# Sharing a score block between the two heads of a pair, split by early and late keys, in a fused linear-attention and MLP kernel

## Chip, cores and metric

The kernel runs on one core of a Trainium2 chip. The metric is device time in microseconds (us). All times quoted are medians of runs in the undisturbed ("fast") state; one run of the kernel before (240.27 us, in the round with the copies on ACT) was slow and is left out of the ratios. The engines are called PE (matrix engine), PEld (its weight loads), DVE (vector engine), ACT (scalar engine), POOL (GpSimd) and SP (which issues transfers).

## The reference

Two stages run one after the other. The first is causal linear attention with a decay per head. The second is a two-layer MLP without biases.

```
# q, k, v: (4, 8, 768, 64)   batch, heads, tokens, width;   lam: one decay per head
# blocks of 64 tokens; rel = i - j
Dmask = where(rel >= 0, lam ** rel, 0)
out   = ((q @ k.T) * Dmask) @ v  +  (q * lam**(pos+1)) @ state     # inside the block + state
state = lam**64 * state + (k * lam**(63-pos)).T @ v
x = attention output as (3072, 512)
h = x @ w_in                                   # 512 -> 2048
g = where(h >= 1, h, where(h <= -1, 0, (h + 1)**2 / 4))
y = g @ w_out                                  # 2048 -> 512
```

## The kernel before

The kernel works in chunks of 128 tokens: 24 chunks, six per batch element. Decay is folded into q and k by tables of `lam**pos` and `lam**-pos` ("casts", mostly on POOL), so that the mask inside a chunk is a plain causal 0/1 mask. Heads are handled in four pairs, since two heads of width 64 fill 128 rows.

For each chunk, PE transposes q and k. DVE copies the transposed k into `kbd`, one 128x128 weight per head, whose other head's rows are zero. PE makes a score block per head (`ps`, two groups of four because only one PSUM bank is free). DVE masks each group (`sc`). PE multiplies with v (`vi`, one weight per head, the other head's columns zero) and adds the state term, all into `po`.

```
def cast_v(c):                               # ACT: v to bf16, straight into the weight layout
    nc.scalar.copy(out=v_out(vi[c % NV]), in_=qkv_ld[c, 2]...)

def f_kb(c, hi):                             # DVE, two per chunk
    nc.vector.tensor_copy(kbd[c % NKB][HD[hi], :, hi, :], ptt[c][HD[hi], 1])

def f_s(c, g):                               # PE, g = 0, 1: 4 matmuls of 128 columns
    pst[c, g] = pp_s.tile([128, 4, 128], F32, ...)           # one buffer
    for j in range(2):
        for hi in range(2):
            nc.tensor.matmul(pst[c, g][:, 2*j+hi, :], lhsT=kbd[c % NKB][:, 2*g+j, hi, :],
                             rhs=qT[c][:, 2*g+j, :], start=True, stop=True)

def f_m(c, g):                               # DVE, mask: 128x512
    nc.vector.tensor_tensor(sc_sb[c][:, 4*g:4*g+4, :], pst[c, g], _bc(causal, 1, 4), op=AX.mult)

def f_o(c):                                  # PE: state term, then two heads, per pair
    for hp in range(HP):
        if cb > 0: nc.tensor.matmul(po[:, hp], lhsT=ubd[...][:, hp, :], rhs=qT[c][:, hp, :], ...)
        for hi in range(2):
            nc.tensor.matmul(po[:, hp], lhsT=vi[c % NV][:, hp, hi]..., rhs=sc_sb[c][:, 2*hp+hi, :], ...)
```

The MLP runs beside this: first layer `ph` on PE, `r` on ACT, three DVE operations `t`, `w`, `gT` on 128x1024, second layer `py` on PE, `osb` on ACT.

Every operation is registered with an engine and a cost in nanoseconds. When the program is built, a list scheduler simulates the engines with these costs and emits each engine's instructions in the simulated order. At run time each engine takes its instructions in that order.

```
add(("kb", c, hi), "DVE", 365, lambda: f_kb(c, hi), needs...)
add(("s", c, h), "PE", mm(*[128] * 4), lambda: f_s(c, h), needs...)     # mm(n) = n / 2.4 + 3 ns
add(("m", c, h), "DVE", 690, lambda: f_m(c, h), needs...)
...                                          # cut: the other operations, loads, weights
run_plan({"PE": 7000, "ACT": 6500, ...})     # simulate, then emit in the simulated order
```

## Time and profile before

| | before |
|---|---|
| median of 3 runs | 238.5 us (238.32 to 239.11) |
| span of the profiled run | 234.8 us |
| PE / DVE / ACT / POOL busy | 213.8 / 160.3 / 123.4 / 59.4 us |

First the page's busy line, and the line of shares, by engine, of the chain that ended last:

```profile
PE 213.8 (91%) x1876; PEld 137.1 (58%) x1904; DVE 160.3 (68%) x274; ACT 123.4 (53%) x216; POOL 59.4 (25%) x64
...
PE 75%; DVE 16%; ACT 3%; DMA 2%; issue 2%; SPq 0%; ACTq 0%
```

The table of windows splits this by time. Each row gives the stretch, its length, and then the busy time (with instruction counts) of PE, PEld, DVE, ACT and POOL, the granted PE clock, the DMA share and the GB/s:

```profile
22.00:30.00 8.00, 6.83 (x59) 4.26 (x58) 3.24 (x6) 4.41 (x9) 0.00 (x0) 1.00 1.10 198
...
46.00:70.00 24.00, 23.84 (x298) 18.61 (x299) 16.56 (x27) 13.00 (x24) 9.98 (x10) 1.00 0.94 199
70.00:94.00 24.00, 22.57 (x329) 19.45 (x331) 23.35 (x43) 16.59 (x32) 14.76 (x13) 1.00 1.06 216
94.00:134.00 40.00, 39.27 (x425) 27.94 (x431) 30.70 (x53) 23.74 (x42) 10.75 (x10) 1.00 0.81 182
134.00:190.00 56.00, 55.58 (x401) 31.47 (x408) 39.80 (x72) 31.06 (x53) 6.13 (x6) 1.00 0.09 34
```

Window length less PE's busy time is PE's idle time: 1.4 us from 70 to 94 us, 0.7 us from 94 to 134 us and 0.4 us from 134 to 190 us. In the first of these DVE is full too (23.35 of 24 us).

The list of waits on PE names engine, waiting group, releaser, total us, times and longest:

```profile
PE ps L252 <- DVE qT L236: 2.5, 3, 1.7
...
PE ps L252 <- DVE sc L258: 0.8, 3, 0.3
```

The second score group of a chunk needs the PSUM bank that the first mask empties, so it waits for DVE. Here that wait is 0.8 us in the whole run.

Last, two kinds of group lines, with count, total busy and mean ns. The first is the mask; the other two are single `t` operations, the first with a cast on POOL beside it, the second with none:

```profile
L258 DVE TENSOR_TENSOR sc<-ps,causal 128x512 bf16<-128x512 f32 x48 | 33.0, 687 | 19.0 <-PE ps L252 18.8
...
L311 DVE TENSOR_SCALAR t_464<-r 128x1024 bf16<-128x1024 bf16 x1 | 1.7, 1661 | 0.0
...
L311 DVE TENSOR_SCALAR t_486<-r 128x1024 bf16<-128x1024 bf16 x1 | 0.4, 420 | 0.0
```

The same operation takes 420 ns or up to 1661 ns. All that take over 450 ns overlap a cast on POOL.

### The profile page before, as it was taken

Reading aid. Unit: us, or ns where it says so; the run is one execution under the profiler, and the core shown is the slowest. Engines: PE = TensorE matmul, PEld = TensorE weight load, DVE = VectorE, ACT = ScalarE, POOL = GpSimd, SP = SyncE. Lnnn points to the kernel's source line nnn. Section 1 sums busy time; section 2 is a strip of 40 time slices with the busy share of each in tenths; the row PEclk is TensorE's granted clock in tenths of the full one; section 3 lists DMA queues with packets and bytes.
Section 4 is the critical chain, followed back from the end, with each engine's and each line's share of the span. In section 5 each row is a group of like instructions: output and inputs, shape, how many; then the busy total and the mean of one; then the engine's idle time right before and its main releaser. Section 6 shows DMA issues by size and latency. Waiting matters only on the chain.

```text
span 234.8 us, 4665 instructions
## 1 busy us (share of the span) xinstructions
PE 213.8 (91%) x1876; PEld 137.1 (58%) x1904; DVE 160.3 (68%) x274; ACT 123.4 (53%) x216; POOL 59.4 (25%) x64
## 2 busy tenths in 40 slices
PE   0487997999997999999999999999999999999993
PEld 0476633575896997777765455555555454444441
DVE  7587399957499999885776876876766835545300
ACT  3456566243577766666566366566455354544110
POOL 6562071061366548303303403302000000000000
PEclk9999999999999999999999999999999999999999
DMA  6999969986999999899993011011011011110212
GB/s 139 220 212 200 192 112 185 196 162 186 247 201 218 227 221 206 191 243 228 230 255 81 19 45 37 12 45 47 0 45 47 0 45 47 45 43 2 92 51 83
DMA packets 82725, 29.67 MB, mean 126 GB/s; under 512 B 75536, under 2 KB 79632, under 8 KB 82704
## 3 DMA queue, kind: packets, MB, share of 16 engines
q1 hardware_dynamic: 78336, 25.17, 48.2%
q0 software_dynamic: 4224, 4.19, 11.1%
q8 instruction: 15, 0.25, 0.4%
q14 instruction: 6, 0.05, 0.1%
q10 hardware_dynamic: 144, 0.00, 0.0%
HBM read 27.27 MB, written 6.29 MB: 143 GB/s over the span
## 4 chain that ended last, share of the span: by engine, by line
PE 75%; DVE 16%; ACT 3%; DMA 2%; issue 2%; SPq 0%; ACTq 0%
PE py L323 33%; PE ph L295 26%; PE ps L252 5%; DVE gT L315 4%; PE pt L229 4%; PE po L268 4%; DMA x2f<-in_v_dram 2%; DVE sc L258 2%; PE pu L242 2%; PE po L265 2%; ACT r L303 1%; DVE kbd_121 L232 1%; PE ph L288 1%; DVE kbd_120 L232 1%; DVE qT L236 1%
## 5 line engine op out<-in xcount | busy, mean ns | idle before, releaser
L303 ACT ACTIVATE r<-ph,one 128x512 bf16<-128x512 f32 x94 | 64.1, 687 | 57.6 <-PE ph L295 40.9
L295 PE MATMUL ph<-xT,w_in_sb 128*128 128x128 bf16 (+1 forms) x744 | 93.1, 269 | 1.0 <-ACT r L303 0.4
L323 PE MATMUL py<-w_out_sb,gT 128*128 128x512 bf16 x364 | 91.5, 379 | 0.9
L295 PEld LDWEIGHTS <-w_in_sb 128*128 128x128 bf16 x752 | 53.0, 98 | 28.0 <-issue 1.4
L323 PEld LDWEIGHTS <-gT 128*128 128x128 bf16 x384 | 35.4, 98 | 33.3 <-DVE gT L315 0.2
L219 POOL TENSOR_TENSOR ks<-x1f,tab_k 128x512 bf16<-128x512 f32 x21 | 24.0, 1141 | 93.0 <-DMA x1f<-in_k_dram 38.9
L258 DVE TENSOR_TENSOR sc<-ps,causal 128x512 bf16<-128x512 f32 x48 | 33.0, 687 | 19.0 <-PE ps L252 18.8
L219 POOL TENSOR_TENSOR qs<-x0f,tab_q 128x512 bf16<-128x512 f32 x23 | 25.8, 1123 | 7.0 <-DMA x0f<-in_q_dram 6.9
L328 ACT COPY osb<-py 128x512 f32<-128x512 f32 x24 | 14.1, 586 | 20.6 <-PE py L323 20.0
L275 ACT CAST xT<-po 128x512 bf16<-128x512 f32 x24 | 14.0, 585 | 11.9 <-PE po L268 11.8
L242 PEld LDWEIGHTS <-ks 128*128 128x128 bf16 x80 | 6.2, 105 | 9.7 <-DVE ks L219 7.1
L229 PE MATMUL pt<-ident,ks 128*128 128x128 bf16 x96 | 10.1, 232 | 0.1
L229 PE MATMUL pt<-ident,qs 128*128 128x128 bf16 x96 | 10.0, 231 | 0.0
L229 PEld LDWEIGHTS <-ks 128*128 128x128 bf16 x96 | 7.7, 106 | 3.3 <-issue 0.3
L252 PE MATMUL ps<-qT,kbd_121 128*128 128x128 bf16 x64 | 6.8, 229 | 3.0 <-DVE qT L236 1.7
L242 PE MATMUL pu<-vi_126,ks 128*128 128x128 bf16 x24 | 2.5, 232 | 7.7 <-ACT vi_126 L223 7.7
L236 DVE COPY qT<-pt 128x512 bf16<-128x512 bf16 x20 | 8.5, 425 | 0.3
L252 PEld LDWEIGHTS <-kbd_121 128*128 128x128 bf16 x64 | 4.9, 102 | 5.8 <-DVE kbd_121 L232 2.6
L252 PE MATMUL ps<-qT,kbd_120 128*128 128x128 bf16 x64 | 6.8, 229 | 1.4 <-ACT qT L236 1.1
L232 DVE COPY kbd_120<-pt 64x512 bf16<-64x512 bf16 x16 | 6.7, 418 | 1.7 <-PE pt L229 0.9
L252 PE MATMUL ps<-qT,kbd_122 128*128 128x128 bf16 x64 | 6.5, 225 | 1.3 <-DVE qT L236 0.8
L252 PEld LDWEIGHTS <-kbd_120 128*128 128x128 bf16 x64 | 4.8, 102 | 3.8 <-DVE kbd_120 L232 1.8
(207 smaller groups left out, 246.4 us busy)
## 6 DMA issues: line engine op xcount, KB each, us to landing
x1f<-in_k_dram SPq DMA_DIRECT2D x24, 256.0 KB, 4.6
x0f<-in_q_dram SPq DMA_DIRECT2D x24, 256.0 KB, 4.8
x2f<-in_v_dram SPq DMA_DIRECT2D x24, 256.0 KB, 4.7
out_dram<-osb SPq DMA_DIRECT2D x24, 256.0 KB, 2.0
w_in_sb<-in_moe_w_in_dram POOLq DMA_DIRECT2D x4, 512.0 KB, 8.3
w_out_sb<-in_moe_w_out_dram POOLq DMA_DIRECT2D x4, 512.0 KB, 8.3
lam_b<-in_lam_dram ACTq DMA_DIRECT2D x1, 4.0 KB, 3.3
```

The source lines that it names most:

```text
L219: eng.tensor_tensor(t, qkv_ld[c, x], _bc(tab[:, c % NCB, :], 2, D), op=AX.mult)
L229: nc.tensor.transpose(out=ptt[c][:, i, hp, :], in_=pair(x[c], hp), identity=ident)
L232: nc.vector.tensor_copy(kbd[c % NKB][HD[hi], :, hi, :], ptt[c][HD[hi], 1])
L236: (nc.scalar.copy if e == "ACT" else nc.vector.tensor_copy)(qT[c], ptt[c][:, 0])
L242: nc.tensor.matmul(pu[0][:, hp, :], lhsT=pair(ks[c], hp), rhs=v_pair(vi[c % NV], hp), start=(c % NCB == 0 and hp == 0), stop=True, skip_gr ...
L252: nc.tensor.matmul(pst[c, g][:, 2 * j + hi, :], lhsT=kbd[c % NKB][:, 2 * g + j, hi, :], rhs=qT[c][:, 2 * g + j, :], start=True, stop=True)
L258: nc.vector.tensor_tensor(sc_sb[c][:, 4 * g:4 * g + 4, :], pst[c, g], _bc(causal, 1, 4), op=AX.mult)
L275: nc.scalar.copy(out=xT[sx][:, :, off:off + C], in_=pot[c])
L295: nc.tensor.matmul(ph[:, j * m:(j + 1) * m], lhsT=w_in_sb[:, ko, (ni + j) * 128:(ni + j + 1) * 128], rhs=xT[s][:, ko, part * m:(part + 1) ...
L303: nc.scalar.activation(out=r_t[grp][:, i, :], in_=ph_t[s, ni, part], func=AF.Relu, bias=one[:, 0:1])
L323: nc.tensor.matmul(py_t[s, ms], lhsT=gT[s][:, ko, ms * 128:(ms + 1) * 128], rhs=w_out_sb[:, ko, :], start=(ko == 0), stop=(ko == FO - 1))
L328: nc.scalar.copy(out=osb[s, ms], in_=py_t[s, ms])
```

## The change

In each causal 128x128 score block, half of the work for the late 64 keys is wasted: the early 64 queries never see them. With one weight per head this can't be skipped, since a weight holds early and late keys together. The change therefore puts the early 64 keys of both heads of a pair into one weight (block-diagonal), and the late 64 keys into another. The late weight then streams only the late 64 queries: 64 columns instead of 128 in four score and four output matmuls per chunk, and a mask of 128x256 instead of 128x512. The number of matmuls stays.

v must be packed in the same way, which moves rows to other partitions. ACT now writes v in its natural order (`vn`), and four DVE copies of 64x256 per chunk build the packed `vi`. The plan costs such a copy at 140 ns.

```
-    kbd = [const.tile([128, HP, 2, 128], BF16, ...
+    kbd = [const.tile([128, HP, 2, 2, D], BF16, ...
+    vn = [const.tile([128, HP, 2, D], BF16, name=f"vn{i}") for i in range(NV)]
     def cast_v(c):
-        nc.scalar.copy(out=v_out(vi[c % NV]), in_=...)
+        nc.scalar.copy(out=vn[c % NV], in_=...)
+
+    def f_vb(c, g, hi):
+        nc.vector.tensor_copy(vi[c % NV][HD[hi], :, g, hi, :], vn[c % NV][HD[g], :, hi, :])
...                                        # cut: f_kb writes the new layout, f_u reads vn, mask constant
     def f_s(c, g):
+        for hp in range(HP):
+            nc.tensor.matmul(pst[c, g][:, hp, :], lhsT=kbd[c % NKB][:, hp, g]...,
+                             rhs=qT[c][:, hp, 64 * g:], start=True, stop=True)
     def f_m(c, g):
+        nc.vector.tensor_tensor(sc_sb[c][g], pst[c, g], _bc(causal[:, 0:128 - 64 * g], 1, HP), op=AX.mult)
     def f_o(c):
+            for g in range(2):
+                nc.tensor.matmul(po[:, hp, 64 * g:], lhsT=vi[c % NV][:, hp, g]..., rhs=sc_sb[c][g][:, hp, :], ...)
+        for i in range(4):
+            add(("vb", c, i), "DVE", 140, lambda c=c, i=i: f_vb(c, i // 2, i % 2), [("cast", c, 2), ("o", c - NV)])
-            add(("s", c, h), "PE", mm(*[128] * 4), ...
+            add(("s", c, h), "PE", mm(*[128 - 64 * h] * 4), ...
-            add(("m", c, h), "DVE", 690, ...
+            add(("m", c, h), "DVE", 690 - 270 * h, ...
-        add(("o", c), "PE", mm(*[128] * (12 if cb else 8)), ...
+        add(("o", c), "PE", mm(*[128] * (8 if cb else 4), *[64] * 4), ...      # and waits for the four copies
```

More of the change, by code (lines that the diff above doesn't have):

```diff
@@ L97 @@
     nc.gpsimd.memset(causal, 1.0)
-    nc.gpsimd.affine_select(
-        out=causal, in_=causal, compare_op=AX.is_ge, fill=0.0,
-        base=0, pattern=[[1, 128]], channel_multiplier=-1)
+    for lo in (0, 64):
+        m = causal[lo:lo + 64, :]
+        nc.gpsimd.affine_select(out=m, in_=m, compare_op=AX.is_ge, fill=0.0,
+                                base=0, pattern=[[1, 128]], channel_multiplier=-1)
     NKB, NUB, NV = 3, 3, 4
-    kbd = [const.tile([128, HP, 2, 128], BF16, name=f"kbd{i}") for i in range(NKB)]
+    kbd = [const.tile([128, HP, 2, 2, D], BF16, name=f"kbd{i}") for i in range(NKB)]
     ubd = [const.tile([128, HP, 128], BF16, name=f"ubd{i}") for i in range(NUB)]
     vi = [const.tile([128, HP, 2, 2, D], BF16, name=f"vi{i}") for i in range(NV)]
+    vn = [const.tile([128, HP, 2, D], BF16, name=f"vn{i}") for i in range(NV)]
     nc.vector.memset(vi[0], 0.0)
@@ L122 @@
         nc.vector.memset(t, 0.0)
-    def v_out(t):
-        a = list(t[:, 0, 0, 0, :].ap)
-        return bass.AP(t.tensor, t[:, 0, 0, 0, :].offset, [a[0], [4 * D, HP], [3 * D, 2], [1, D]])
-    def v_pair(t, hp):
-        x = t[:, hp, 0, 0, :]
-        return bass.AP(t.tensor, x.offset, [list(x.ap)[0], [3 * D, 2], [1, D]])
     w_in_sb = big.tile([128, KO, d_ff], BF16)
@@ L222, in cast_v @@
     def cast_v(c):
-        nc.scalar.copy(out=v_out(vi[c % NV]), in_=qkv_ld[c, 2].rearrange("p (a b) d -> p a b d", b=2))
+        nc.scalar.copy(out=vn[c % NV], in_=qkv_ld[c, 2].rearrange("p (a b) d -> p a b d", b=2))
+    def f_vb(c, g, hi):
+        nc.vector.tensor_copy(vi[c % NV][HD[hi], :, g, hi, :], vn[c % NV][HD[g], :, hi, :])
     def f_t(c):
@@ L231, in f_kb @@
     def f_kb(c, hi):
-        nc.vector.tensor_copy(kbd[c % NKB][HD[hi], :, hi, :], ptt[c][HD[hi], 1])
+        nc.vector.tensor_copy(kbd[c % NKB][HD[hi], :, :, hi, :], ptt[c][HD[hi], 1].rearrange("p a (b d) -> p a b d", b=2))
     def f_qT(c, e):
@@ L241, in f_u @@
         for hp in range(HP):
-            nc.tensor.matmul(pu[0][:, hp, :], lhsT=pair(ks[c], hp), rhs=v_pair(vi[c % NV], hp),
+            nc.tensor.matmul(pu[0][:, hp, :], lhsT=pair(ks[c], hp), rhs=vn[c % NV][:, hp].rearrange("p a d -> p (a d)"),
                              start=(c % NCB == 0 and hp == 0), stop=True, skip_group_check=True)
@@ L248, in f_s @@
     def f_s(c, g):
-        pst[c, g] = pp_s.tile([128, 4, 128], F32, name="ps", tag="ps")
-        for j in range(2):
-            for hi in range(2):
-                nc.tensor.matmul(pst[c, g][:, 2 * j + hi, :], lhsT=kbd[c % NKB][:, 2 * g + j, hi, :],
-                                 rhs=qT[c][:, 2 * g + j, :], start=True, stop=True)
+        t = pp_s.tile([128, 4, 128], F32, name="ps", tag="ps")
+        pst[c, g] = t if g == 0 else t[:, 0:2, :].rearrange("p a (b d) -> p (a b) d", b=2)
+        for hp in range(HP):
+            nc.tensor.matmul(pst[c, g][:, hp, :], lhsT=kbd[c % NKB][:, hp, g].rearrange("p a d -> p (a d)"),
+                             rhs=qT[c][:, hp, 64 * g:], start=True, stop=True)
     def f_m(c, g):
         if g == 0:
-            sc_sb[c] = scp.tile([128, 2 * HP, 128], BF16, name="sc", tag="sc")
-        nc.vector.tensor_tensor(sc_sb[c][:, 4 * g:4 * g + 4, :], pst[c, g], _bc(causal, 1, 4), op=AX.mult)
+            sc_sb[c] = [scp.tile([128, HP, n], BF16, name=f"sc{n}", tag=f"sc{n}") for n in (128, 64)]
+        nc.vector.tensor_tensor(sc_sb[c][g], pst[c, g], _bc(causal[:, 0:128 - 64 * g], 1, HP), op=AX.mult)
     def f_o(c):
@@ L266, in f_o @@
                                  start=True, stop=False)
-            for hi in range(2):
-                nc.tensor.matmul(po[:, hp], lhsT=vi[c % NV][:, hp, hi].rearrange("p a d -> p (a d)"),
-                                 rhs=sc_sb[c][:, 2 * hp + hi, :], start=(cb == 0 and hi == 0), stop=(hi == 1))
+            for g in range(2):
+                nc.tensor.matmul(po[:, hp, 64 * g:], lhsT=vi[c % NV][:, hp, g].rearrange("p a d -> p (a d)"),
+                                 rhs=sc_sb[c][g][:, hp, :], start=(cb == 0 and g == 0), stop=(g == 1))
     def f_x(c):
@@ L408 @@
         for h in range(2):
-            add(("s", c, h), "PE", mm(*[128] * 4), lambda c=c, h=h: f_s(c, h),
+            add(("s", c, h), "PE", mm(*[128 - 64 * h] * 4), lambda c=c, h=h: f_s(c, h),
                 [("kb", c, 0), ("kb", c, 1), ("qT", c), ("m", c, 0) if h else ("m", c - 1, 1)],
                 due=od - 3000 + 1000 * h, extra=FILL)
-            add(("m", c, h), "DVE", 690, lambda c=c, h=h: f_m(c, h), [("s", c, h), ("o", c - 3), ("m", c, 0) if h else None])
-        add(("o", c), "PE", mm(*[128] * (12 if cb else 8)), lambda c=c: f_o(c),
-            [("m", c, 1), ("cast", c, 2), ("ub", c - 1, 0) if cb else None, ("ub", c - 1, 1) if cb else None,
+            add(("m", c, h), "DVE", 690 - 270 * h, lambda c=c, h=h: f_m(c, h), [("s", c, h), ("o", c - 3), ("m", c, 0) if h else None])
+        add(("o", c), "PE", mm(*[128] * (8 if cb else 4), *[64] * 4), lambda c=c: f_o(c),
+            [("m", c, 1), *(("vb", c, i) for i in range(4)), ("ub", c - 1, 0) if cb else None, ("ub", c - 1, 1) if cb else None,
              ("x", c - 1), ("o", c - 1)], due=od, extra=FILL)
```

## The prediction

> **What bounds the kernel now.** The page's busy table gives PE 213.8 us of a 234.8 us span (91%), DVE 160.3 (68%), ACT 123.4, POOL 59.4; the chain that ended last is 75% PE and 16% DVE. By the window table: from 0 to 30 us a serial chain of loads, DVE, ACT and small matmuls fills the first four chunks. From 30 to 46 us DVE is the limit (15.5 of 16 us; PE loses 2.0). From 46 to 70 us PE is full. From 70 to 94 us both are nearly full: DVE 23.4 of 24 us, PE 22.6. From 94 us on PE is the limit (98 to 99%) and DVE has 15 to 40% slack.
>
> **Removed.** Per chunk the four late score matmuls and the four late output matmuls stream 64 columns instead of 128, and the late mask goes from 128x512 to 128x256. The mask takes 687 ns now, of which 512 elements at one per cycle are 533; I estimate 420 ns, so DVE saves 0.27 us x 24 = 6.4 us. Counts of matmuls and weight loads stay; 192 matmuls are halved. In the timeline a warm 128-column matmul with its own weights comes every 55 ns. If 64 columns came every 29 ns, PE would save 192 x 27 ns = 5.1 us. But each has a new 128-column weight load. The Trainium skill (TensorE: Matmul & The Clock Gate, LDWEIGHTS) says load time goes with the column count. In this trace a lone load takes 0.15 us early, where matmuls come every 105 ns, and 0.10 us later at 55 ns: the difference fits 128 columns at one per cycle. So it is likely (60%) that loads hold the rate near 50 ns and save nearly nothing. Expected: 2 us.
>
> **Added.** Four DVE copies of 64x256 bf16 per chunk, SBUF to SBUF, 96 in all. The SBUF-to-SBUF tensor_scalar of 1024 bf16 takes 420 ns, 267 of it at four per cycle (the skill, VectorE: DVE Perf Modes, tier table: copies too). A copy is then an estimated 67 + 150 = 0.22 us, not the 0.14 in the kernel's plan; 96 make 21 us. Beside running POOL work such DVE operations stretch (420 to as much as 1660 ns in the groups): 2 to 4 us more. DVE rises by about 17 us, to near 177.
>
> **Moved.** The output matmuls also wait for the copies. Before about 130 us some score, transpose and output groups change places on PE.
>
> **On the critical path.** Startup: 3.5 us of copies, 1 us of mask less, partly in the chain: +1.2 us. From 30 to 46 us: +0.7. From 70 to 94 us, six or seven chunks at +0.7 us of DVE where DVE is already full: about +3. From 94 us on the copies are hidden, and only the PE saving counts. Sum: +4.9 - 2 = about +3 us.
>
> **Prediction: 241.5 us**, range 236.5 to 247.5. Chances: faster by over 2% 0.06, within 2% 0.62, slower by over 2% 0.32.
>
> **What would show it.** Right: copies near 0.22 us and late masks near 0.42; DVE busy 172 to 182 us; PE idle growing between 70 and 94 us with PE waiting for DVE; a run of 64-column matmuls spaced near 50 ns. Wrong: 64-column spacing near 29 ns, PE busy down by 5 us; DVE idle still above 1 us from 70 to 94.
>
> **What would make it wrong.** Faster: 64-column matmuls really take half, and copies overlap each other. Slower: contention with POOL delays casts and so loads, or the new PE order puts matmuls behind late DVE results.

## The result, and the profile after

| | before | after |
|---|---|---|
| median | 238.41 us (4 runs) | 250.03 us (4 runs, 249.46 to 251.63) |
| ratio | | 1.0491 (95% interval 1.0428 to 1.0555) |
| span of the profiled run | 234.8 us | 247.8 us |
| DVE busy | 160.3 us | 183.8 us |

A ratio here and below is the mean time of one kernel's fast runs over the mean of the other's in the same rounds, so it is not quite the ratio of the medians. The change made the kernel 11.6 us slower, outside the predicted range.

The page's busy line and the chain's shares after the change:

```profile
PE 213.3 (86%) x1877; PEld 132.6 (54%) x1904; DVE 183.8 (74%) x370; ACT 122.9 (50%) x216; POOL 62.8 (25%) x65
...
PE 45%; DVE 45%; ACT 3%; issue 2%; DMA 2%; SPq 0%; ACTq 0%
```

DVE's share of the chain went from 16% to 45%. The windows after:

```profile
22.00:30.00 8.00, 7.09 (x57) 4.81 (x55) 2.00 (x6) 1.74 (x4) 0.00 (x0) 0.61 1.01 176
...
46.00:70.00 24.00, 22.95 (x263) 16.45 (x265) 18.59 (x37) 10.38 (x18) 8.69 (x8) 1.00 0.78 171
70.00:94.00 24.00, 18.31 (x287) 15.98 (x285) 23.34 (x48) 14.88 (x29) 13.94 (x12) 1.00 1.14 209
94.00:134.00 40.00, 34.95 (x444) 26.89 (x452) 37.92 (x83) 21.86 (x40) 10.96 (x9) 1.00 0.79 175
134.00:190.00 56.00, 54.13 (x389) 29.46 (x396) 46.89 (x91) 30.64 (x54) 10.76 (x10) 1.00 0.18 50
```

DVE is now full from 70 to 134 us (61.3 of 64 us), and PE idles 5.7, 5.1 and 1.9 us in the last three rows, against 1.4, 0.7 and 0.4 us. From 22 to 30 us the granted clock is 0.61: PE ran at half clock for 6.8 us there.

The waits on PE show the new stop:

```profile
PE ps L246 <- DVE sc L252: 10.4, 14, 1.6
...
PE ps L246 <- DVE qT L230: 3.9, 3, 1.7
PE ps L246 <- DVE kbd L226: 2.0, 2, 1.6
PE po L262 <- DVE sc L252: 1.8, 4, 0.9
```

The wait of 0.8 us became 10.4 us, in 14 waits. The DVE groups, split by shape, show the copies and the two masks:

```profile
L217 DVE COPY vi<-vn 64x256 bf16<-64x256 bf16 x96 | 32.6, 339 | 2.8 <-ACT vn L214 1.7
...
L252 DVE TENSOR_TENSOR sc<-ps,causal 128x512 bf16<-128x512 f32 x24 | 16.5, 687 | 4.4 <-PE ps L246 4.0
L252 DVE TENSOR_TENSOR sc<-ps,causal 128x256 bf16<-128x256 f32 x24 | 10.0, 417 | 2.2 <-PE ps L246 2.1
```

The short mask takes 417 ns, as estimated. The copies have a minimum of 207 ns and a median of 222 ns, also as estimated, but a mean of 339 ns. Counted in the trace, 71 of the 96 overlap no cast on POOL and take 231 ns on average (three of these take 357 to 568 ns, beside POOL's issuing of weight transfers between 14 and 19 us); the 25 that do overlap a cast take 648 ns.

A stretch of the timeline (start, length, instruction, in brackets the idle time before it and its releaser) shows one such case with its consequence:

```profile
135.45 2.44 DVE L217 COPY vi<-vn 64x256 bf16<-64x256 bf16 x4
...
135.77 1.04 POOL L210 TENSOR_TENSOR ks<-x1f,tab_k 128x512 bf16<-128x512 f32 x1 [7.93 <-issue]
...
136.34 0.39 PE L246 MATMUL ps<-qT,kbd 128*128 128x128 bf16 x4
...
136.77 1.04 POOL L210 TENSOR_TENSOR qs<-x0f,tab_q 128x512 bf16<-128x512 f32 x1
...
137.93 0.69 DVE L252 TENSOR_TENSOR sc<-ps,causal 128x512 bf16<-128x512 f32 x1
...
138.67 0.28 PE L246 MATMUL ps<-qT,kbd 128*128 128x64 bf16 x4 [0.22 <-DVE sc L252]
```

Four copies take 2.44 us instead of 0.9. Singly, the first two take 0.22 us each and the last two 0.99 us each, and each of those last two ends less than 0.1 us after a cast on POOL ends. The mask stands behind them in DVE's queue, and starts 1.2 us after its scores are there (136.34 + 0.39 us). The second score group then holds up PE, by 0.22 us here.

The same lines show the part that the prediction doubted. Four matmuls of 64 columns take 0.28 us from first start to last end, against 0.39 us for four of 128 columns. The single starts in the trace are 28 to 29 ns apart, against 55 ns. So a matmul of half the width takes half the time here, with a new 128-column weight for each.

Progress can be read from the weight loads of the second-layer matmuls, whose number (384) is the same in both. The first one starts at 40.5 us before and 44.5 us after. The hundredth or so (about 100 us) is 9.9 us late, the hundred-and-fiftieth about 12.5 us, and from there on the lateness stays. The loss thus comes in three pieces: about 4 us up to the first one, about 6 us from 60 to 100 us, and 2.5 us from there to 135 us.

### The profile page after: what moved, and what is told of

The parts are those of the page before. It is cut to its first block, busy times and chain, and to the rows that moved or that the text cites. A ratio compares the mean times of both kernels' runs of the same rounds, so it can differ in the third digit from the quotient of the medians.

```text
span 247.8 us, 4763 instructions
## 1 busy us (share of the span) xinstructions
PE 213.3 (86%) x1877; PEld 132.6 (54%) x1904; DVE 183.8 (74%) x370; ACT 122.9 (50%) x216; POOL 62.8 (25%) x65
## 4 chain that ended last, share of the span: by engine, by line
PE 45%; DVE 45%; ACT 3%; issue 2%; DMA 2%; SPq 0%; ACTq 0%
PE py L317 22%; PE ph L289 15%; DVE vi L217 11%; DVE gT L309 8%; DVE w L307 7%; DVE sc L252 6%; DVE kbd L226 5%; DVE t L305 4%; DVE qT L230 2%; DMA x2f<-in_v_dram 2%; PE pt L223 2%; PE ps L246 2%; ACT r L297 2%; PE po L262 1%; PE ph L282 1%
## 5 line engine op out<-in xcount | busy, mean ns | idle before, releaser
L305 DVE TENSOR_SCALAR t<-r 128x1024 bf16<-128x1024 bf16 x48 | 22.3, 464 | 30.2 <-ACT r L297 29.9
L309 DVE TENSOR_TENSOR gT<-w,t 128x1024 bf16<-128x1024 bf16 x48 | 39.0, 812 | 1.7
L307 DVE TENSOR_TENSOR w<-r,t 128x1024 bf16<-128x1024 bf16 x48 | 36.1, 752 | 1.7
L217 DVE COPY vi<-vn 64x256 bf16<-64x256 bf16 x96 | 32.6, 339 | 2.8 <-ACT vn L214 1.7
L252 DVE TENSOR_TENSOR sc<-ps,causal 128x512 bf16<-128x512 f32 (+1 forms) x48 | 26.5, 552 | 6.6 <-PE ps L246 6.1
L210 POOL TENSOR_TENSOR qs<-x0f,tab_q 128x512 bf16<-128x512 f32 x23 | 28.1, 1222 | 12.5 <-DMA x0f<-in_q_dram 12.2
L246 PE MATMUL ps<-qT,kbd 128*128 128x128 bf16 (+1 forms) x192 | 16.8, 212 | 16.4 <-DVE sc L252 10.4
L226 DVE COPY kbd<-pt 64x512 bf16<-64x512 bf16 x48 | 20.1, 418 | 1.7 <-ACT qT L230 0.7
L262 PE MATMUL po<-sc,vi 128*128 128x128 bf16 x192 | 18.5, 214 | 1.9 <-DVE sc L252 1.8
L240 ACT CAST ubd<-pu 64x256 bf16<-64x256 f32 x40 | 14.6, 366 | 4.7 <-PE pu L236 4.3
L214 ACT CAST vn<-x2f 128x512 bf16<-128x512 f32 x24 | 14.9, 619 | 3.6 <-DMA x2f<-in_v_dram 3.6
```

The costliest lines, as they stand in the source:

```text
L210: eng.tensor_tensor(t, qkv_ld[c, x], _bc(tab[:, c % NCB, :], 2, D), op=AX.mult)
L217: nc.vector.tensor_copy(vi[c % NV][HD[hi], :, g, hi, :], vn[c % NV][HD[g], :, hi, :])
L226: nc.vector.tensor_copy(kbd[c % NKB][HD[hi], :, :, hi, :], ptt[c][HD[hi], 1].rearrange("p a (b d) -> p a b d", b=2))
L246: nc.tensor.matmul(pst[c, g][:, hp, :], lhsT=kbd[c % NKB][:, hp, g].rearrange("p a d -> p (a d)"), rhs=qT[c][:, hp, 64 * g:], start=True, ...
L252: nc.vector.tensor_tensor(sc_sb[c][g], pst[c, g], _bc(causal[:, 0:128 - 64 * g], 1, HP), op=AX.mult)
L262: nc.tensor.matmul(po[:, hp, 64 * g:], lhsT=vi[c % NV][:, hp, g].rearrange("p a d -> p (a d)"), rhs=sc_sb[c][g][:, hp, :], start=(cb == 0 ...
```

## The experiments

Theory A: the copies on DVE cost the time, through their own length, their stretch beside POOL, and the PE queue that waits behind. Rival B: the new order on PE costs it. Rival C: the half-clock stretch costs it. Later a fourth came up, D: the plan's cost for a copy is wrong, and the order made with it is bad for that reason.

### The change without its copies (`e1_no_copies`)

```
     def f_vb(c, g, hi):
-        nc.vector.tensor_copy(vi[c % NV][HD[hi], :, g, hi, :], vn[c % NV][HD[g], :, hi, :])
+        pass
```

> The changed kernel with the same plan and the same instruction order, but the 96 DVE copies are not emitted (the output is wrong on purpose: the packed v stays zero). Theory A, the copies on DVE cost the time: with them gone, DVE busy falls by 33 us to about 151 us, the half-width matmuls and masks pay, and the time is 232 to 236 us, below the 238.4 of before. Rival B, the new order of the score, transpose and output groups on PE costs the time: still 245 us or more. Rival C, the half-clock stretch after startup costs it: it depends on the startup, so 240 to 246 us if the half clock is still there, and the stretch shows in the granted clock.

Measured: 233.12 us against 237.88 for before, ratio 0.9784 (0.9734 to 0.9834). PE's busy time is 207.9 us against 213.8. Every queue has the same order, and the order costs nothing by itself: rival B falls. In the profiled run there is no half-clock stretch after the startup. The halved matmuls and masks are worth 4.8 us, close to the 5.1 us that 192 times 27 ns give; but 1.4 us of it is there already at the first second-layer matmul (39.2 us against 40.5 us), so part of the agreement is chance. The copies cost 16.9 us (250.0 - 233.1).

### Copies in the first four chunks only (`e2_first4`)

```
+        if c < NV:
             nc.vector.tensor_copy(vi[c % NV]...)
```

> As the run without copies, but the 16 copies of the first four chunks are kept (wrong output on purpose). It separates the startup from the rest. If the copies cost about the 4 us that the first output-layer matmul was late, here too: 3 to 4.5 us above the run without copies, and with the half-clock stretch. If the startup loss is made up later by slack on PE: under 1 us above it.

Measured: 237.10 us, ratio to before 0.9958 (0.9884 to 1.0033), and 4.0 us above the run without copies. So 16 copies in the startup chain cost 4.0 us, and the other 80 cost 12.9 us. In the profiled run the half clock is back (from 21.8 to 28.6 us), so it goes with these copies. The Trainium skill (TensorE: Matmul & The Clock Gate, Part 1) says that PE's clock is granted by recent activity. The trace agrees. The records of the clock begin with full clock at 14.55 us in the changed kernel and at 14.51 us in the run without copies. These are the windows from there, the changed kernel first:

```profile
14.55:21.38 6.83, 3.45 (x53) 2.65 (x51) 6.28 (x15) 3.18 (x7) 4.05 (x5) 1.00 1.22 191
...
14.51:21.34 6.83, 4.88 (x73) 3.73 (x71) 5.19 (x11) 4.63 (x10) 4.15 (x5) 1.00 1.25 197
```

Half clock follows where PE was busy 3.45 us (and 3.58 us in this run), and not where it was busy 4.88 us. The table of windows must be read with care here: it counts time before the first clock record as full clock. In the kernel before, that record is at 19.1 us, and the matmuls come every 106 to 107 ns until then and every 55 to 56 ns after. So that kernel too ran at half clock, for its first 19.1 us; the changed kernel did until 14.6 us and then again for 6.8 us. That second stretch can have delayed PE by at most 3.4 us (an estimate: half of 6.8 us). Rival C is thus part of this 4.0 us, not separate from A; how the 4.0 us divide between the two was not measured.

### Order alone, and copies alone (`e3_order_only`, `e4_wide_copies`)

Both keep the plan of the changed kernel, so its order, but take the full-width functions of before. The second adds 96 copies of the same shape into a tile that nothing reads.

```
     def f_vb(c, g, hi):
+        pass                                                                   # e3
+        nc.vector.tensor_copy(vd[c % NV][HD[hi], :, g, hi, :], vi[c % NV][HD[g], :, hi, hi, :])   # e4
```

> The work of before (full-width score, mask and output, no copies) in the plan and the order of the changed kernel. Theory A: the order matters little, 237 to 241 us. Rival B, the order is at fault: 245 us or more.

> The work of before in the order of the changed kernel, plus 96 copies of the same shape and strides at the same places of the DVE queue, into a tile that nothing reads. Theory A: DVE busy rises by 30 to 35 us over the run with the order alone, to about 193 us, and the time by more than the 11.6 us of the real change since here DVE does not get the shorter masks: 252 to 260 us. If it was not DVE time but the wait of the output matmuls for the copies (nothing waits for these): 240 to 245 us.

Measured: 237.59 us (0.9964, 0.9908 to 1.002) and 254.49 us (1.0707, 1.0637 to 1.0777). The order alone costs nothing. Copies on which no matmul waits cost 16.9 us, as much as those of the real change. So it is the time they take in DVE's queue that counts, not the new wait of the output matmuls. PE's wait for the mask is 10.4 us in this run too:

```profile
PE ps L256 <- DVE sc L262: 10.4, 14, 1.7
```

### Copies on ACT, and as transfers (`e5_act_copies`, `e7_dma_copies`)

```
-        nc.vector.tensor_copy(...)
+        nc.scalar.copy(...)           # e5, 380 ns in the plan
+        nc.scalar.dma_start(...)      # e7, 60 ns on ACT and 2.5 us to landing in the plan
```

> The changed kernel with its 96 copies on ACT instead of DVE (and costed so in the plan, at 380 ns). If DVE time is the cause and ACT has room (123 us busy of 248), the stalls between 60 and 130 us go and the time is 233 to 239 us, with DVE busy near 151 us and ACT near 160 us, and no copy stretched by POOL. If the copies only change the queue that is full, because each output group waits for ACT's copies and ACT also drains the h and y banks: 243 us or more.

> The 96 copies as transfers from SBUF to SBUF, issued from ACT's queue right after the cast of v. DVE busy as without copies (about 155 us). If only engine time matters: 232 to 237 us. If the small rows (128 bytes) crowd the 16 DMA engines while the loads are still running (to about 130 us): loads land later and the time is 238 to 250 us.

On ACT: 237.68 us, ratio 0.9961 (0.9883 to 1.004), so the loss is gone, but so is the gain. A copy takes 403 ns there and ACT becomes nearly full: 36.9 of 40 us from 94 to 134 us. As transfers: 266.69 us, ratio 1.1184. This missed both expectations. A copy landed 4.2 us after its issue, and the first second-layer matmul came 15 us late. It was not followed further.

### Short casts on POOL (`e10_short_casts`, `e11_short_casts_before`)

From the fifth chunk on, POOL casts one head of eight. The same edit is made in the kernel before as a control.

```
+        t = fix[x][c % 3]                       # fixed tiles, so that the rest holds older values
+        n = H if eng is nc.vector or c < 4 else 1
-        eng.tensor_tensor(t, qkv_ld[c, x], ...)
+        eng.tensor_tensor(t[:, 0:n, :], qkv_ld[c, x][:, 0:n, :], ...)
```

> The changed kernel, but from the fifth chunk on POOL casts only one head of eight (wrong output on purpose)[...]. The copies on DVE stay. If the stretch of the copies beside POOL (mean 339 ns against 222 ns) carries much of the loss: copies fall to a mean near 235 ns, DVE busy by 15 us or more, and the gap to the same edit of the kernel before falls from 11.6 us to 4 to 8 us. If the plain copies carry it: the gap stays above 9 us.

> The control for the run with short casts: the kernel before with the same edit (wrong output on purpose). POOL work is shorter, the stretched DVE operations (about 9 us over 144 of them) get their plain times, and since PE is nearly full the time falls by 0 to 3 us, to 235.5 to 238.5 us.

Measured: 235.83 us with the change and 233.47 us without it. The gap fell from 11.6 to 2.4 us, less than expected of either theory. The control missed as well: it gained about 5 us instead of 0 to 3, so POOL's casts cost the kernel before something too. The group line of the copies:

```profile
L218 DVE COPY vi<-vn 64x256 bf16<-64x256 bf16 x96 | 22.4, 234 | 3.1 <-ACT vn L215 1.8
```

The mean is 234 ns, and DVE's busy time 163.7 us. The Trainium skill (GPSIMD Engine Reference, Key points) says that POOL shares its SBUF interfaces with DVE and contends with DVE instructions that use both ports or two SBUF inputs. The trace agrees: in the changed kernel the masks and `kbd` copies, which read PSUM, keep their length beside a cast (`kbd` 419 ns without and 418 ns with one, the short mask 418 and 413 ns), while the SBUF copies go from 231 to 648 ns.

### The same, with every copy emitted twice (`e12_double_copies`)

```
+        for _ in range(2 if c >= 4 else 1):
             nc.vector.tensor_copy(vi[c % NV]...)
```

> The run with short casts of the changed kernel, and from the fifth chunk on every copy is emitted twice (wrong output, as there). POOL hardly disturbs DVE here, but DVE is as busy as in the real change: 164 + 80 x 0.23 = about 182 us. If what counts is DVE's total time in the stages where it is full, whatever fills it: 241 to 247 us, most of the 9 us comes back over the 235.8 us of single copies. If it was something else about POOL (casts finishing late, buffers freed late), which this run lacks: 235 to 239 us.

Measured: 251.12 us, ratio to before 1.0554 (1.0485 to 1.0623), above the expected range. POOL disturbs nothing here, DVE is busy 181.9 us, and the loss is back. So the loss doesn't need POOL: under this plan, DVE as full as in the real change is enough. (The plan still has 140 ns for each pair of copies, which takes 462 ns.)

### The plan's cost of a copy (`e9_replan`, `e14_plan230`, `e15_plan440`)

One number of the changed kernel is changed. The result stays right.

```
-            add(("vb", c, i), "DVE", 140, ...
+            add(("vb", c, i), "DVE", 340, ...      # e9;  230 in e14, 440 in e15
```

> The changed kernel with one number changed: the plan costs a copy at 340 ns, as measured, instead of 140. If the loss came from an order that was planned on a wrong cost: 238 to 245 us. If the copies' time itself is too much for DVE whatever the order: 246 to 252 us.

> The changed kernel, the copy costed at 230 ns in the plan: its length without POOL beside it. If the loss shrinks steadily as the plan's cost nears the measured mean of 340 ns: 242 to 247 us, between 250.0 (140 ns) and 240.7 (340 ns). If the 340 ns run was a lucky order: anywhere from 238 to 252 us, not between the two.

> The changed kernel, the copy costed at 440 ns in the plan, more than measured. If the plan only has to leave enough room for the copies: 238 to 243 us. If orders are a lottery: 245 us or more is as likely.

| cost in the plan | time | ratio to before | mean length of a copy | DVE busy | PE waits for `sc` before `ps` |
|---|---|---|---|---|---|
| 140 ns (the change) | 250.03 us | 1.0491 | 339 ns | 183.8 us | 10.4 us |
| 230 ns | 246.00 us | 1.0347 | 336 ns | 182.9 us | 6.8 us |
| 340 ns | 240.69 us | 1.0139 | 305 ns | 179.7 us | 1.3 us |
| 440 ns | 238.88 us | 1.0070 | 317 ns | 185.0 us | 4.1 us |

The run with 340 ns, the first of these to be made, was a surprise: with the same copies, the loss falls from 4.9% to 1.4%. That is 8.4 us by the ratios (9.3 us between the medians, but the kernel before was 1.3 us faster in that round), and 2.1 us of it is there at the first second-layer matmul (42.4 us against 44.5 us). The other two speak against a lucky order. The time falls as the plan leaves more room, while the copies and DVE's busy time hardly change. The last step, from 340 to 440 ns, lies within the scatter (1.0066 to 1.0211 and 1.0016 to 1.0123). The wait in the last column does not fall with it, so it is no measure of the loss by itself. In the run with 340 ns, the window from 94 to 134 us and the wait are:

```profile
94.00:134.00 40.00, 39.48 (x475) 29.11 (x479) 38.53 (x84) 25.55 (x48) 12.35 (x12) 1.00 0.96 209
```

```profile
PE ps L246 <- DVE sc L252: 1.3, 3, 0.6
```

DVE is as full as in the changed kernel (38.5 against 37.9 of 40 us), yet PE loses 0.5 us instead of 5.1. A full DVE is thus not enough to stop PE. PE stops when its queue reaches a chunk's matmul before DVE is ready, and the plan decides when that is.

### The startup's copies, and later ones, on ACT (`e16_start_act`, `e17_late_act`)

```
+        (nc.scalar.copy if c < CPS else nc.vector.tensor_copy)(...)                    # e16
+        (nc.scalar.copy if c < CPS or c >= 3 * CPS else nc.vector.tensor_copy)(...)    # e17
+            add(("vb", c, i), *(("ACT", 400) if ... else ("DVE", 340)), ...
```

> The copies of the first four chunks are on ACT (400 ns in the plan), all others on DVE at 340 ns in the plan. The first output-layer matmul was 1.9 us late in the run with 340 ns; if those copies are the cause, it comes 1 us before that of the kernel before, and the time is 236.5 to 239 us. If the startup is made up later anyway: 239.5 to 241.5 us.

> As the run before this one, but the copies from the thirteenth chunk on are on ACT as well; DVE keeps those of the eight chunks in the middle. If DVE's stretch beside POOL after 94 us still costs something: 235 to 237.5 us, the fastest of the versions that compute the right result. If it costs nothing there: equal to that run within 1 us.

Measured: 238.27 us (1.0048, 1.0012 to 1.0085) and 238.83 us (1.0043, 1.0000 to 1.0086). With the first four chunks' copies on ACT, the first second-layer matmul starts at 40.0 us, 0.6 us earlier than before, and the total is in the expected range. Moving the late ones as well brought nothing.

### Shared and padded versions (`e13_mix`, `e18_mix_padded`, `e19_act_padded`, `e20_before_padded`)

`e13` puts the copies of the first four and the last eight chunks on ACT and shares the others, two and two. `e18` is the same with higher costs in the plan, `e19` is the version with all copies on ACT with higher costs, and `e20` is the kernel before with its chunk operations on DVE costed higher, as a control.

```
+    def vb_act(c, g): return g == 1 or not CPS <= c < 4 * CPS
+            add(("vb", c, i), *(("ACT", 400) if vb_act(c, i // 2) else ("DVE", 300)), ...   # e13; 500 and 440 in e18
+            add(("vb", c, i), "ACT", 500, ...                                                # e19
+            add(("kb", c, hi), "DVE", 460, ...     # e20, was 365; qT likewise, the mask 760 instead of 690
```

> A version meant to be faster: the copies of the first four chunks and of those from the seventeenth on are on ACT, those between are shared, two on DVE and two on ACT. If both full queues of the middle stage are relieved: 233 to 236.5 us, below before and below the version with all copies on ACT (237.7). If the middle stage has no room on either engine: 237 to 241 us.

> The shared version (first four and late chunks on ACT, two and two between), with the copies costed at 500 ns on ACT and 440 ns on DVE in the plan, more than measured. If room in the plan is what the shared version still lacks: 233.5 to 236 us, faster than the kernel before by about 1%. If not: 236 to 238.5 us.

> All copies on ACT, costed at 500 ns in the plan instead of 380 (403 measured). If room in the plan helps: 234 to 237 us. If ACT is simply full between 70 and 130 us: 237 to 239 us.

> The control for the plan's costs: the kernel before, with its chunk operations on DVE costed about 70 to 95 ns longer in the plan (the same 0.4 us per chunk that going from 140 to 230 ns gives the copies). If the gain from an honest plan belongs to the copies: 237 to 240 us, as before. If a roomier plan helps any version: 233 to 236 us.

Measured, with the ratio to before: `e13` 237.20 us (0.9967, 0.9899 to 1.0034), `e18` 238.55 us (1.0002, 0.9954 to 1.0051), `e19` 241.59 us (1.0156, 1.0118 to 1.0195), `e20` 237.34 us (0.9986, 0.9935 to 1.0036). The control shows that extra room doesn't help a plan in general; it helps where a real cost was left out, and hurt the version with all copies on ACT. No version that computes the right result beat the kernel before beyond the noise. The bound is the run without copies: they would have to become free to gain 4.8 us.

## Why the prediction was wrong

The direction, slower, was the prediction's median, but its size was +3 us where +11.6 us came, and the range ended at 247.5 us. Point by point:

- **Length of the copies and masks: right when alone.** "A copy is then an estimated 67 + 150 = 0.22 us": the median is 222 ns. Late mask: 417 ns for an estimated 420.
- **Stretch beside POOL: named, but mis-sized.** "2 to 4 us more" was 11.3 us for the copies (32.6 us less 96 times 0.222). The prediction took the effect from operations of 0.42 us and more, of which 31 in 144 met a cast. It did not reckon that a copy, however short, can be held until a cast of about 1 us ends (one took 1.08 us). DVE rose by 23.5 us instead of 17.
- **"... it is likely (60%) that loads hold the rate near 50 ns and save nearly nothing": wrong.** The spacing is 28 to 29 ns and the saving 4.8 us (run without copies), which made the error of the sum smaller. The inference rested on how long lone weight loads take in two clock states, which says nothing of how closely they follow each other.
- **"Startup ... +1.2 us", "From 30 to 46 us: +0.7": mis-sized.** Together 4.0 us, shown by the first second-layer matmul and by the run with the first four chunks' copies alone. The second stretch of half clock was not foreseen.
- **"From 70 to 94 us ... about +3": mis-sized.** The second-layer matmuls fell back by 6 us between about 60 and 100 us.
- **"From 94 us on the copies are hidden": this step failed.** It counted DVE's idle time from 94 us on (15 to 40%) as room for the copies. But DVE came out of the stretch before late, stayed full to 134 us, and PE's queue was already fixed. PE lost 5.1 us from 94 to 134 us, where the prediction had none.
- **The term that was mis-sized** is the sum of the critical path, "+4.9": the copies cost 16.9 us (run without copies; again 16.9 us with the wide matmuls). The missing mechanism is the plan. The prediction saw that the plan costs a copy at 140 ns and that this is too little, but used this only to cost the copies. It did not follow it into the order, although it listed "the new PE order puts matmuls behind late DVE results" among the things that would make it wrong. The same copies with 340 or 440 ns in the plan cost 8.4 and 10.0 us less, by the ratios.

The copies' time on DVE and the plan's wrong cost are both needed for the loss: without the copies the order is harmless (runs `e1` and `e3`), and with honest costs the copies nearly are. How the loss divides between them can't be given as a sum, because taking away either one nearly removes it. One thing stays open: in the run with 230 ns a copy exceeds its cost in the plan by 106 ns, in that with short casts by 94 ns, yet they end 8.4 us and 2.4 us above their controls. In the former the MLP's DVE operations are stretched by POOL too, which no plan here accounts for, but that this makes the whole difference was not shown.

## What to carry to other kernels

When an order is planned from costs, an added operation must be entered at its measured length with its neighbours running, not at its length alone; before you judge such a change, vary that one cost and see whether the time moves. A gain on the busiest engine that is paid for on an engine that is full in even one stage must be judged there, and the idle time of later stages counts as room only if the queue order lets work move into it. To learn what a new helper operation costs, run the change without it at the same order (wrong result), and the old kernel with it: here both gave 16.9 us, closer than the scatter of the runs.

## What the Trainium skill lacked or had wrong

- *TensorE: Matmul & The Clock Gate* (Back-to-back issue gap) names about 81 ns for a sustained stream of load and matmul pairs at 128 columns. Here 128-column matmuls, each with a new weight, start 55 to 56 ns apart, and 64-column ones 28 to 29 ns apart; the section's formula for an isolated matmul (columns over 2.4, and 2.5) fits both.
- The same page (LDWEIGHTS) gives a weight load's length as the column count over 1.2, which is 107 ns for 128 columns, whatever the clock. In the kernel before, most such loads take 147 to 152 ns while matmuls come every 107 ns, and 95 to 98 ns later. Neither length sets the rate of the matmuls above.
- The same page (Part 1) ties the drop of the clock to an idle window of about 3.4 us, and doesn't say what share of busy time keeps the clock. In the changed kernel it was halved after 6.83 us in which PE was busy 3.45 us and waited 1.5 us at the longest; in the run without copies, with 4.88 us busy, it stayed.
